# Logits of two router layers with their matrix as the weights on four column groups, and an earlier load of the memory matrix

## The chip, the cores and the metric

One NeuronCore of a Trainium2 chip runs the whole program. The metric is the time of one execution in microseconds on the device; lower is better. TensorE (PE in the rows, its weight loads PEld) multiplies, VectorE (DVE) and ScalarE (ACT) empty PSUM and do the element work, GpSimd (POOL) works on SBUF alone, and SyncE (SP) issues most DMAs.

## What is computed

An attention with a memory read, then two mixture-of-experts layers, each with one expert for a token. All is float32. There are 4 batches of 576 positions, 8 heads of width 64, so 2304 tokens of width 512, 8 experts with a hidden width of 1024.

```python
a = softmax(causal(q @ k.T / 8));  local = a @ v
q_p = where(q > 0, q, exp(q) - 1) + 1
mem = (q_p @ M_prev) / (q_p @ z_prev + 1e-6)
x = g * mem + (1 - g) * local            # g = sigmoid(beta), per head

def moe(x, l, w1, w2):                   # l: the logits of 8 experts
    e = argmax(l, axis=1); gate = softmax(l)[e]
    return gate * (relu(x @ w1[e]) @ w2[e])
# layer 1: l = (x/|x|) @ (emb/|emb|).T / tau;   layer 2: l = x @ w_gate
```

## The kernel before, in words

**Attention.** The work goes by 16 pairs of heads (4 batches times 4 pairs), each cut into 10 units. A loop over units writes out by hand what every engine does in each of them; tables of events (`ev_pe` for TensorE, `ev_ew` for the others) are filled ahead with functions under unit numbers, 10 units to a pair. Within a unit the elementwise events come before the scores, these before the TensorE events. Every engine runs its own instructions in the order written, so that a place in a table is a place in each queue. `load_mz` (line 76) puts the memory matrix and its normalizer into the tile `mz`: a GpSimd memset and four DMAs on SP. It stands under unit -4. `scale_v` (line 108) multiplies the first pair's values by 1 - g on GpSimd, under unit -7, and has to wait for their DMA and for the gate. `mscale` (line 174) then scales the first pair's block of `mz` on GpSimd, and `M` (line 181) is the matmul with it into `psm`.

**Logits of the first layer.** While a later pair is computed, the finished rows of a batch are transposed to `xT` (four blocks of 128 features, by 512 or 640 tokens). For batches 0 to 2 `lg_pe` (line 1054) forms their logits: for each tile of 128 tokens (4, 5 and 4 of them) four matmuls, one for each block of features, with the block of `xT` as the weights (128 by 128) and 8 columns of the scaled matrix `enT` streaming. They are put in two places, units 10 and 11 behind a batch's base. The last batch is done apart (`part_pe`, `last`) and is not touched.

**The experts.** A step is one tile of up to 128 rows of one expert. `step` (line 1342) writes it by hand: a first product into `ph0` and `ph1`, a ReLU, transposes (`hT`), a second product into `py` (24 matmuls). Operands are split in a high and a low float32r part (`hilo`: an ACT copy and a DVE subtraction), weights too (`splits`), whenever the next expert's weights come in. In a step of the first layer TensorE also routes the rows that the step before has put out: `yT_pe` (line 1269) transposes them into `pm0`, `yT_ev` copies them to `hs[0]` on ACT, `logits_pe` (line 1264) makes their logits of the second layer with four matmuls (again the rows as weights, 8 columns of `wgT` streaming), and `route2` turns these into an expert and a gate on DVE. Between the layers `chain1` (line 1615) does the same for the last step, interleaved with the first step of the second layer by the numbers in `n1`.

## Time and profile before

| | us |
|---|---|
| median of 3 runs (lowest, highest) | 925.56 (925.24, 927.02) |
| profiled execution, its own time | 926.38 |
| its span, first to last instruction | 924.6 |
| TensorE busy in it | 894.5 (97%) |
| VectorE, ScalarE, GpSimd busy | 494.9, 482.3, 269.8 |

The profile follows one execution. A busy share is an average over the whole span, so stretches are read apart: the timeline gives the start and length of single instructions or of runs of equal ones, a view by stretches gives the busy time of every engine and the granted clock of TensorE (1.00 is 2.4 GHz, 0.50 is 1.2 GHz). A float32 matmul that is no transposition stands in the records as two weight loads and two matmuls.

### The profile page before, as it was taken

The numbers are of one execution on the slowest core, as the hardware profiler recorded it, in microseconds if no ns is written. First come the engines' busy times: TensorE is split into PE (matmuls) and PEld (weight loads), VectorE is DVE, ScalarE is ACT, GpSimd is POOL, SyncE is SP. The second block draws the span as 40 slices with busy tenths as digits, with TensorE's granted clock in tenths as the row PEclk, the third lists the DMA queues.
The fourth block names the chain that finished last, engine by engine and source line by source line (L and its number), as shares of the span: only waits on it lengthen the run. The fifth ranks groups of instructions, "written<-read, shape, count | busy, mean of one in ns | idle before, by whom it ended". The sixth has DMA issues, their size and how long they took to land. (4 is left out here: it accounts for less than half of the span.)

```text
span 924.6 us, 20884 instructions
## 1 busy us (share of the span) xinstructions
PE 894.5 (97%) x5351; PEld 713.9 (77%) x5351; DVE 494.9 (54%) x1563; ACT 482.3 (52%) x969; POOL 269.8 (29%) x370
## 2 busy tenths in 40 slices
PE   5999999999999999999999999998999999999996
PEld 2777777787777878887888888886868888888885
DVE  3565675556575685369635576543567314463430
ACT  3566666646755835467434463532266434564531
POOL 3364744526434102211222212121131212221221
PEclk9899999979999999999999999999999999999999
DMA  6311433413305245438523416111657514384111
GB/s 130 73 41 40 124 115 90 121 21 72 86 14 195 80 148 201 133 116 303 174 96 115 139 47 207 60 48 39 228 193 277 186 47 130 121 298 144 42 36 39
DMA packets 102437, 110.31 MB, mean 119 GB/s; under 512 B 69882, under 2 KB 69882, under 8 KB 102276
## 3 DMA queue, kind: packets, MB, share of 16 engines
q1 hardware_dynamic: 94244, 85.33, 30.3%
q0 software_dynamic: 8032, 23.22, 7.6%
q8 instruction: 54, 0.88, 0.4%
q14 instruction: 107, 0.88, 0.3%
HBM read 90.32 MB, written 19.25 MB: 119 GB/s over the span
## 5 line engine op out<-in xcount | busy, mean ns | idle before, releaser
L1226 PE MATMUL py<-Wh,b 128*128 (+1 forms) x688 | 243.3, 409 | 2.2 <-DVE b L1170 2.1
L1226 PE MATMUL ph<-Wh,b 128*128 (+1 forms) x672 | 230.6, 404 | 0.6 <-ACTq L1237 0.6
L920 DVE TENSOR_TENSOR Wl<-stg,Wh 128x1024 f32 (+1 forms) x120 | 145.3, 1224 | 87.1 <-ACT Wh L917 81.4
L1226 PEld LDWEIGHTS py<-Wh,b 128*128 128x128 f32 x688 | 129.5, 188 | 30.0 <-DVE b L1170 3.7
L1226 PEld LDWEIGHTS ph<-Wh,b 128*128 128x128 f32 x672 | 126.9, 189 | 29.7 <-ACTq L1237 1.0
L917 ACT ACTIVATE Wh<-stg 128x1024 f32 (+1 forms) x120 | 125.7, 1058 | 23.8 <-DVEq L1237 7.5
L1226 PE MATMUL py<-Wl,b 128*128 (+1 forms) x344 | 135.8, 395 | 0.0
L1226 PE MATMUL ph<-Wl,b 128*128 (+1 forms) x336 | 133.4, 397 | 1.2 <-DVEq L1237 1.2
L1170 DVE TENSOR_TENSOR b<-pt,b 128x512 fp32r<-128x512 f32 x86 | 59.4, 690 | 112.4 <-ACT b L1169 112.0
L287 ACT ACTIVATE att<-psat 128x512 f32<-128x512 f32 (+1 forms) x144 | 66.7, 463 | 88.5 <-PE psat L285 87.6
L308 PE MATMUL psav<-vb,att 128*128 128x128 f32 (+1 forms) x640 | 96.6, 282 | 0.9 <-ACT att L287 0.8
L308 PEld LDWEIGHTS psav<-vb,att 128*128 128x128 f32 x640 | 81.8, 192 | 12.4 <-issue 4.3
L1325 POOL DMA_INDIRECT out_dram<-ysb,xca x21 | 25.8, 1231 | 196.4 <-ACTq L1237 126.1
L1169 ACT ACTIVATE b<-pt 128x512 fp32r<-128x512 f32 x86 | 51.6, 600 | 53.8 <-PE pt L1330 41.3
L1226 PEld LDWEIGHTS ph<-Wl,b 128*128 128x128 f32 x336 | 63.7, 190 | 14.7 <-DVEq L1237 1.7
L1320 ACT ACTIVATE ysb<-py,xca 128x512 f32<-128x512 f32 x42 | 28.8, 687 | 88.1 <-PE py L1226 72.0
L1226 PEld LDWEIGHTS py<-Wl,b 128*128 128x128 f32 x344 | 65.0, 189 | 10.7
L233 DVE CUSTOM_DVE_ANT_0 a<-pss,wmask 128x128 f32<-128x128 f32 (+3 forms) x128 | 61.0, 485 | 21.4 <-PE pss L255 11.0
L268 ACT ACTIVATE a<-a,mx 128x128 f32<-128x128 f32 (+3 forms) x128 | 71.1, 556 | 0.4 <-DVE mx L233 0.3
L1135 POOL DMA_INDIRECT xg<-x_scratch,idx x48 | 55.2, 1150 | 39.2 <-POOL xca L1314 11.1
L1436 POOL DMA_DIRECT2D x_scratch<-xcb x21 | 11.9, 564 | 170.2 <-DVEq L1237 63.5
L285 PE MATMUL psat<-ident,a 128*128 128x128 f32 x320 | 58.1, 280 | 0.2
(370 smaller groups left out, 1309.1 us busy)
## 6 DMA issues: line engine op xcount, KB each, us to landing
stg<-in_moe_w_dram SPq DMA_DIRECT2D x120, 512.0 KB, 4.7
x_scratch<-ysb POOLq DMA_DIRECT2D x22, 256.0 KB, 2.7
qkn<-in_q_dram SPq DMA_DIRECT2D x32, 128.0 KB, 2.8
qkn<-in_k_dram SPq DMA_DIRECT2D x32, 128.0 KB, 2.9
vb<-in_v_dram SPq DMA_DIRECT2D x32, 128.0 KB, 2.6
x_scratch<-xb SPq DMA_DIRECT2D x16, 256.0 KB, 4.2
x_scratch<-stg SPq DMA_DIRECT2D x11, 258.0 KB, 3.0
xg<-x_scratch,idx POOLq DMA_INDIRECT x48, 4.1
```

What stands on the lines that cost most here:

```text
L233: nc.vector.tensor_tensor_reduce(out=out, in0=ps, in1=mask, scale=1.0, scalar=bound, op0=ALU.add, op1=ALU.min, accum_out=m)
L268: nc.scalar.activation(out=a[:, 0:N], in_=a[:, 0:N], func=AF.Exp, scale=-1.0, bias=mx, accum_out=rs_t[pi][:, c, j:j + 1])
L285: nc.tensor.transpose(ps[:, 128 * i:128 * i + 128], x, ident)
L287: nc.scalar.activation(out=att[:, 0:N], in_=ps[:, 0:N], func=AF.Copy)
L308: nc.tensor.matmul(av_t[pi][:, c, j:], att[:, 128 * kb:128 * kb + 128], vn[:, kb, j:, 0:D], start=(kb == 0), stop=(kb == c))
L917: return nc.scalar.activation(out=chunk(Wh, c, wv), in_=stg[:, c].unsqueeze(1), func=AF.Copy).ins
L920: return nc.vector.tensor_tensor(out=chunk(Wl, c, wv), in0=stg[:, c].unsqueeze(1), in1=chunk(Wh, c, wv).bitcast(F32), op=ALU.subtract).ins
L1135: return nc.gpsimd.indirect_dma_start(out=rows_of(t), out_offset=None, in_=rows, in_offset=bass.IndirectOffsetOnAxis(ap=idx[:, L, t:t + 1] ...
L1169: nc.scalar.activation(out=hi, in_=ps, func=AF.Copy)
L1170: nc.vector.tensor_tensor(out=lo, in0=ps, in1=hi.bitcast(F32), op=ALU.subtract)
L1226: mm = nc.tensor.matmul(ps, x[:, col:col + P], W, start=(first and q_ == qs[0]), stop=(last and q_ == qs[-1]))
L1320: nc.scalar.activation(out=ysb, in_=py, func=AF.Copy, scale=xc[:, 0:1])
```

## The change

Three things change. The tile `sel` (128 by 8) is new: a matrix of zeros with ones at rows 40 kk + e of column e, made once by five small GpSimd instructions in `setup_gates`.

First, both logits are made in two stages. The matrix, all four blocks of features by 8 experts (32 columns), is now the weights, and the rows stream: block kk of the rows (512 columns in the attention, 128 in a step) goes into the 32 PSUM partitions from 32 kk on. The 128 partitions so hold four times four parts, of which sel picks the four that belong, after they have been copied back to SBUF (ACT in the attention, over block 0 of `xT`; DVE in a step, over the first 128 columns of the transposed rows). A second matmul with that as weights and `sel` streaming adds them up. The fifth tile of batch 1 keeps the old way.

Second, in a step the transposes of the rows and their copy move ahead of the second half of the first product. Third, `load_mz` goes from unit -4 to unit -8.

```diff
-    ev_ew.setdefault(-4, []).append(load_mz)
+    ev_ew.setdefault(-8, []).append(load_mz)
...
+            nc.gpsimd.memset(sel, 0.0)
+            for kk in range(KD):
+                nc.gpsimd.affine_select(out=sel, in_=sel, pattern=[[-1, E]], compare_op=ALU.not_equal, fill=1.0, base=-(KD + 1) * E * kk, channel_multiplier=1)
...
-                sp = 2
-                for i in range(sp):
-                    pe(base + d - sp + i, lambda b=b, i=i, n=r.n: self.lg_pe(b, slot("pslg") if i == 0 else self.ps["lg"], tiles=range(i, n, sp)))
+                pe(base + d - 4, lambda b=b: self.parts_pe(b, slot("pslp")))
+                ew(base + d - 3, lambda b=b: self.parts_ev(b))
+                pe(base + d - 1, lambda b=b: self.sum_pe(b, slot("pslg")))
...
+        def parts_pe(self, b, ps):
+            self.ps["lp"] = ps
+            g = KD * E
+            for n in range(KD):
+                nc.tensor.matmul(ps[g * n:g * n + g], enT.rearrange("p k e -> p (k e)"), self.xT[b][:, n, 0:512], start=True, stop=True)
+        def parts_ev(self, b):
+            cp(1, self.xT[b][:, 0, 0:512], self.ps["lp"])
+        def sum_pe(self, b, ps):
+            self.ps["lg"] = ps
+            for i in range(4):
+                nc.tensor.matmul(ps[:, E * i:E * i + E], self.xT[b][:, 0, P * i:P * i + P], sel, start=True, stop=True)
+            if self.cols(b)[1] == 5:
+                self.lg_pe(b, ps, tiles=(4,))
...
+    def parts_pe(yT):
+        for kk in range(KD):
+            nc.tensor.matmul(pm0[KD * E * kk:KD * E * kk + KD * E, 0:P], wgT.rearrange("p k e -> p (k e)"), yT[:, P * kk:P * kk + P], start=True, stop=True)
+    def parts_ev(yT):
+        nc.vector.tensor_copy(yT[:, 0:P], pm0[:, 0:P])
     def logits_pe(yT):
-        for kk in range(KD):
-            nc.tensor.matmul(pm1[:, 0:E], yT[:, P * kk:P * kk + P], wgT[:, kk], start=(kk == 0), stop=(kk == KD - 1))
+        nc.tensor.matmul(pm1[:, 0:E], yT[:, 0:P], sel, start=True, stop=True)
...
         hT(0, b)
+        if rt2:
+            yT_pe()
+            yT_ev(b.hs[0])
...
-            next_rows(t + 1)
+            xT_pe(rows_of(t + 1))
         if rt2:
-            yT_pe()
-            yT_ev(b.hs[0])
+            parts_pe(b.hs[0])
+            parts_ev(b.hs[0])
+        if more:
+            hilo(psx, b.x)
+        if rt2:
             route2_iov()
...
         yield
+        parts_pe(b.hs[1])
+        parts_ev(b.hs[1])
+        yield
         logits_pe(b.hs[1])
...
-    C, n1 = chain1(), (1, 1, 1, 5, 1, 0, 2, 0, 4, 6, 0)
+    C, n1 = chain1(), (1, 1, 1, 6, 1, 0, 2, 0, 4, 6, 0)
```

Line numbers in the lists of the changed kernel are its own. First the SP queue from the first pair's values on (`vb`: values, `qkn`: queries and keys), before:

```order
L105 DMA vb_141<-in_v_dram 128x4x64 x2
L106 DMA vb_141<-in_v_dram 64x2x64
L105 DMA vb_142<-in_v_dram 128x4x64 x2
L106 DMA vb_142<-in_v_dram 64x2x64
L96 DMA qkn<-in_q_dram 128x4x64 x2
L96 DMA qkn<-in_k_dram 128x4x64 x2
L98 DMA qkn<-in_q_dram 64x2x64
L98 DMA qkn<-in_k_dram 64x2x64
L84 DMA mz<-in_M_prev_dram 64x16x64
L85 DMA mz<-in_z_prev_dram 64x16x1
L84 DMA mz<-in_M_prev_dram 64x16x64
L85 DMA mz<-in_z_prev_dram 64x16x1
```

The same stretch of the SP queue now:

```order
L105 DMA vb_142<-in_v_dram 128x4x64 x2
L106 DMA vb_142<-in_v_dram 64x2x64
L84 DMA mz<-in_M_prev_dram 64x16x64
L85 DMA mz<-in_z_prev_dram 64x16x1
L84 DMA mz<-in_M_prev_dram 64x16x64
L85 DMA mz<-in_z_prev_dram 64x16x1
L105 DMA vb_143<-in_v_dram 128x4x64 x2
L106 DMA vb_143<-in_v_dram 64x2x64
L96 DMA qkn<-in_q_dram 128x4x64 x2
L96 DMA qkn<-in_k_dram 128x4x64 x2
L98 DMA qkn<-in_q_dram 64x2x64
L98 DMA qkn<-in_k_dram 64x2x64
```

The four loads of `mz` pass the nine issues for pairs 1 and 2; on GpSimd their memset passes the first pair's `scale_v` likewise. Next TensorE in the attention, where batch 0 has its logits (`pst`, `pstr`: transposes of queries and keys, `psat`: of the weights of attention, `psm`: memory, `pss`: scores), before:

```order
L285 MATMUL psat<-ident,al_146 128x128 x4
L255 MATMUL pss<-kT,qT 128x512 x2
L136 MATMUL pst<-ident,qkn 128x128 x4
L1060 MATMUL pslg<-enT,xT 128x8 x8
L285 MATMUL psat<-ident,a 128x128
L285 MATMUL psat<-ident,al_146 128x128
L185 MATMUL psm<-mz,ph 128x130 x3
L1060 MATMUL pslg<-enT,xT 128x8 x8
L285 MATMUL psat<-ident,a 128x128
```

And now, from two units further ahead:

```order
L1074 MATMUL pslp<-xT,enT 32x512 x4
L308 MATMUL psav<-vb_144,att 128x128 x2
L185 MATMUL psm<-mz,ph 128x130
L185 MATMUL psm<-mz,ph 64x130
L308 MATMUL psav<-vb_144,att 128x64 x2
L285 MATMUL psat<-ident,al_147 128x128 x4
L255 MATMUL pss<-kT,qT 128x512 x2
L136 MATMUL pst<-ident,qkn 128x128 x4
L285 MATMUL psat<-ident,a 128x128
L285 MATMUL psat<-ident,al_147 128x128
L185 MATMUL psm<-mz,ph 128x130 x3
L1083 MATMUL pslg<-sel,xT 128x8 x4
```

Sixteen matmuls with 8 columns have become four with 512 columns onto 32 partitions each, right behind the transposes of `pstr`, and four with 8 columns. Last TensorE in a step of the first layer (`psx`: the next rows' transposes, `pm`: the tiles `pm0` and `pm1`, `hs`: transposed rows), before:

```order
L1226 MATMUL ph_4146<-Wh_4137,b_4238 128x512
L1165 MATMUL psx<-ident,xg_4235 128x128 x4
L1271 MATMUL pm_4150<-ident,ysb 128x128 x4
L1226 MATMUL py<-Wh_4138,b_4239 128x512
L1226 MATMUL py<-Wl_4140,b_4239 128x512
L1226 MATMUL py<-Wh_4138,b_4240 128x512
L1330 MATMUL pt_4148<-ident,hs_4233 128x128 x4
L1226 MATMUL py<-Wh_4138,b_4239 128x512
L1226 MATMUL py<-Wl_4140,b_4239 128x512
L1226 MATMUL py<-Wh_4138,b_4240 128x512
L1267 MATMUL pm_4145<-wgT,hs_4232 128x8 x4
L1226 MATMUL py<-Wh_4138,b_4239 128x512
```

And now:

```order
L1250 MATMUL ph_4142<-Wh_4133,b_4234 128x512
L1189 MATMUL psx<-ident,xg_4231 128x128 x4
L1292 MATMUL pm_4146<-hs_4228,wgT 32x128 x4
L1250 MATMUL py<-Wh_4134,b_4235 128x512
L1250 MATMUL py<-Wl_4136,b_4235 128x512
L1250 MATMUL py<-Wh_4134,b_4236 128x512
L1362 MATMUL pt_4144<-ident,hs_4229 128x128 x4
L1250 MATMUL py<-Wh_4134,b_4235 128x512
L1250 MATMUL py<-Wl_4136,b_4235 128x512
L1250 MATMUL py<-Wh_4134,b_4236 128x512
L1299 MATMUL pm_4141<-sel,hs_4228 128x8
L1250 MATMUL py<-Wh_4134,b_4235 128x512
```

The place of the rows' transposes (L1271) is taken by the four matmuls with 32 output partitions; the transposes themselves now stand six matmuls earlier, behind the first `hT`. At the old place of the logits one matmul is left of four.

## Rows read from the trace of the kernel before

**Rows 1.** The page, part 1: busy time of the engines, share of the span, instructions.
```profile
PE 894.5 (97%) x5351; PEld 713.9 (77%) x5351; DVE 494.9 (54%) x1563; ACT 482.3 (52%) x969; POOL 269.8 (29%) x370
```

**Rows 2.** Timeline of the start: us from the start, length, engine, line, operation, count [idle before, releaser].
```profile
14.71 1.82 POOL L78 MEMSET mz<- 128x2080 f32 x1
22.97 0.40 POOL L177 TENSOR_TENSOR mz<-mz,gt 128x128 f32<-128x128 f32 x1 [6.43 <-DMA mz<-in_M_prev_dram]
...
10.29 1.15 SPq L105 DMA_DIRECT2D vb<-in_v_dram  x2
...
18.76 1.06 SPq L85 DMA_DIRECT2D mz<-in_z_prev_dram  x1
...
18.80 0.38 PE L285 MATMUL psat<-ident,al 128*128 128x128 f32 x1
23.42 1.43 PE L185 MATMUL psm<-mz,ph 128*128 128x130 f32 x4 [4.24 <-POOL mz L177]
```

**Rows 3.** Stretches: us, busy (count) of PE, PEld, DVE, ACT, POOL, granted clock, DMA, GB/s.
```profile
22.43:29.25 6.82, 5.83 (x30) 3.84 (x30) 2.79 (x11) 0.98 (x3) 2.53 (x3) 0.50 0.62 131
114.59:118.00 3.41, 3.41 (x22) 2.32 (x22) 2.25 (x8) 1.10 (x4) 1.78 (x3) 0.50 0.00 0
186.27:196.51 10.24, 10.24 (x55) 8.82 (x54) 4.29 (x19) 2.91 (x9) 3.86 (x5) 0.50 0.03 6
```

**Rows 4.** Timeline of TensorE at the logits of attention's batches 0, 1 and 2.
```profile
109.95 1.92 PE L1060 MATMUL pslg<-enT,xT 128*128 128x8 f32 x16
...
119.78 0.49 PE L255 MATMUL pss<-kT,qT 64*128 64x256 f32 x2
...
183.11 2.74 PE L1060 MATMUL pslg<-enT,xT 128*128 128x8 f32 x24
...
196.95 0.70 PE L255 MATMUL pss<-kT,qT 64*128 64x256 f32 x4
...
259.25 1.92 PE L1060 MATMUL pslg<-enT,xT 128*128 128x8 f32 x16
...
267.57 0.70 PE L255 MATMUL pss<-kT,qT 64*128 64x256 f32 x4
```

**Rows 5.** Timeline of TensorE in one step, and all matmuls of L1267 (minimum, median, maximum ns).
```profile
396.06 0.40 PE L1226 MATMUL py<-Wh,b 128*128 x1
396.29 0.95 PE L1267 MATMUL pm<-wgT,hs 128*128 128x8 f32 x8
397.10 0.48 PE L1226 MATMUL py<-Wh,b 128*128 x1
397.42 0.39 PE L1226 MATMUL py<-Wl,b 128*128 x1
...
L1267 PE MATMUL pm<-wgT,hs x176: 170/256/256, 339.4 to 638.5; 128*128 128x8 f32 x176
```

**Rows 6.** Timeline of TensorE where scores of two heads run; 64*128: rows by columns used.
```profile
160.64 0.27 PE L285 MATMUL psat<-ident,a 128*128 128x128 f32 x1
...
160.84 0.49 PE L255 MATMUL pss<-kT,qT 64*128 64x128 f32 x4
161.16 0.22 PE L152 MATMUL pstr<-ident,qkn 64*128 64x64 f32 x1
...
156.66 0.46 PE L244 MATMUL pss<-kT,qT 64*64 64x288 f32 x2
...
156.96 0.41 PE L244 MATMUL pss<-kT,qT 64*64 64x288 f32 x2
157.30 0.33 PE L1039 MATMUL psxt<-ident,xb 128*128 128x128 f32 x1
```

**Rows 7.** All copies of the transposed rows on ScalarE (minimum, median, maximum ns).
```profile
L1274 ACT ACTIVATE hs<-pm x22: 598/604/607, 337.8 to 636.4; 128x512 f32<-128x512 f32 x22
```

**Rows 8.** Timeline between the layers: the first hT's low part, the ranks.
```profile
641.39 0.69 DVE L1170 TENSOR_TENSOR b<-pt,b 128x512 fp32r<-128x512 f32 x1 [1.55 <-ACT b L1169]
...
641.96 0.18 PE L1303 MATMUL pm<-oh,tri 128*128 128x8 bf16 x1
```

More of the change, by code (lines that the diff above doesn't have):

```diff
@@ L525, in tile_kernel @@
     wgT = cst.tile([P, KD, E], F32, name="wgT")
+    sel = cst.tile([P, E], F32, name="sel")
     rtau = cst.tile([P, 1], F32, name="rtau")
```

## The prediction

> **What bounds the kernel now.** I read the page's busy times first, then TensorE's idle times by releaser, then the granted clock by stretches, then the timeline around each edit. TensorE is busy 894.5 of 924.6 us [rows 1]. So an edit is worth what it takes off TensorE's queue, unless it falls into one of the few idle times, and work moved to the other engines, each busy half the time, is free as long as nobody waits for it. The largest idle time is at the start: 4.24 us before the first matmul with `mz`, released by the scaling of `mz` on GpSimd [rows 2]. Right behind it the clock is low: 0.50 of 2.4 GHz from 22.43 to 29.25 [rows 3]. Two more low stretches lie right behind the logits of batches 0 and 1: 3.41 us and 10.24 us [rows 3]. Behind those of batch 2, the same code, it stays high.
>
> **The earlier load of `mz`.** The scaling at 22.97 waited for a DMA, of which the last was issued at 18.76 [rows 2]: 4.2 us from issue to use. These issues stood behind nine others for pairs 1 and 2 that begin at 10.29, and behind the memset, which ran at 14.71 to 16.53 because it came after the first pair's scaling of values. Now the memset comes first; GpSimd has nothing else then and the values land later anyway, so it costs nothing there. The four issues begin near 10.3 and end near 13.5 (the sequence took 3.3 us with its gaps: 16.5 to 19.8). With 4.2 us to use, `mz` is scaled at some 17, and TensorE wants it at 19.2. The stall of 4.24 us goes, with 2 us to spare. What is late next: loads of pairs 1 and 2 come 3.3 us later, but pair 1's values are first used some 10 us behind this point, pair 2's queries later still. Bounds: 3.0 gained if the small packets of `mz` and the other loads delay each other by 3 us more, 4.24 if not. I take 4.2.
>
> The clock adds to it. TensorE stood still for most of 19.2 to 23.4, and the low stretch followed. Without the stall it has work throughout. In 22.43 to 29.25 it was busy for 5.83 us at half speed [rows 3]; at full speed that is 2.9 less. DVE and ACT then have to keep up with twice the pace directly, so I take 2.0, bounds 0 and 2.9. Sum of this edit: -6.2.
>
> **What one logits matmul costs now.** In a step two matmuls of the second product start at 396.06 and 396.29, 0.23 apart; with eight records of the logits behind, the next two start at 397.10 and 397.42 [rows 5]. 397.42 - 396.06 less two intervals of 0.23 is 0.90 us: 0.112 for each record. Eight columns don't take that long; the load of 128 weight columns does. In the attention sixteen records from 109.95 on take the same per record [rows 4].
>
> **What streaming costs.** No row shows column groups side by side; the nearest are the scores, where two heads use different halves of the array [rows 6]. Four records of 128 columns from 160.84 to 161.16 take 0.32; two of 288 take 0.30 (156.66 to 156.96), and the second of each two starts within 0.01 of the first: two lengths ("x2, 0.46") that one record alone would have. Solving both: 0.11 us for 128 streamed columns, 0.43 for 512, 0.10 for a load of 128 weight columns, 0.05 for 64, and so some 0.03 for 32. Also: between a transposition (0.11 itself) and the first of these pass 0.20, and 0.34 from the last pair of 288 (0.25 itself) to the next transposition: 0.09 for each change of the array's form.
>
> **A step.** Two records stay for the last matmul, 0.22; saved 0.67. The four new matmuls, if the groups run side by side in two rounds: 0.09 + 0.03 + 2 x 0.11 + 0.02 of stagger + 0.09, and the next weights' load in the open, 0.11: 0.56. Net -0.11, and 176 records are 22 such places [rows 5], 21 of them in steps: -2.3. If groups run one after another it is eight rounds for two, +0.66, net +0.55.
>
> DVE's copy of 128 columns is below ACT's 0.60 for 512 [rows 7]; between it and its reader stand six matmuls and four transposes of TensorE, 6 x 0.23 + 0.4 = 1.8 us, so it is hidden. The moved transposes cost TensorE the same. Their ACT copy now stands between the high part of the first `hT` and the ReLU of `ph1`: both copies are 0.60 each, some 1.6 with the hand-overs, while TensorE has the four transposes, six matmuls and the next rows' transposes, 2.3. Hidden with 0.7 to spare, less in steps where ACT also copies weights; there I allow 0 to 0.5 each. Queued behind that copy is only the ReLU, which has to wait for `ph1` anyway.
>
> **Between the layers.** Here the logits come half a product later than before. Ranks start at 641.96, and DVE spends 641.39 to 642.08 on the low part of the first `hT` [rows 8]; the second half of the expert's choice now falls behind that. TensorE would wait until about 642.5. With 0.34 more for the matmuls less what is saved: +0.5 in place of -0.1, bounds 0 and 1.
>
> **The attention.** Batch 0 had 32 records, 3.58. Now `pslp` stands behind `pstr`, which already has its own form, so that one change of form is new: 0.09 + 0.03 + 2 x 0.43 + 0.02 = 1.00; then eight records, 0.90. Saved 1.68, the same for batch 1 (its fifth tile stays) and 2: -5.0. Side by side or not decides here too: eight rounds for two are +2.6 a batch. ACT's new copy, 0.60 [rows 7], comes three times beside other work; the added PSUM buffer is freed by it two units before its next user. The five small GpSimd instructions stand on no path.
>
> From the first logits to the same score matmul pass 8.32 us in batch 2, 9.83 in batch 0 and 13.84 in batch 1 [rows 4]; batch 1 has eight records more, 0.90. So the low clock costs 1.5 and 4.6 us. What TensorE did before each fall was long series of 8-column matmuls. In their place come 0.9 us of streaming and half or less of these; batch 2 had as much and kept its clock. I take -5.0 of the 6.1, bounds 0 and 6.1.
>
> The Trainium skill speaks of such groups twice, and the sum above uses neither. TensorEngine Tiling (Array Packing), Key Properties, says that tiles work independently, weight loads too; TensorE: Matmul & The Clock Gate, Measured speedup vs the span model, has 2.38 times for three column tiles. As an estimate from that page, four groups would take 2.5 rounds, not 2: 910 in place of 908. No row here can show it.
>
> **Sum.** -6.2 - 5.0 - 5.0 - 2.3 + 0.5 = -18.0. The profiled execution took 926.4, so 908.4; it is 0.8 over the median of the runs, so 907.6 to 908 for a median.
>
> **Rivals.**
>
> Groups in order of the program. Each float32 matmul is two records. If a group may start only when the group before has begun its second record, four matmuls take five rounds, not two: +0.33 in 22 places is 7.3, +1.3 in three is 3.9: 919. Against it: with two heads the second one's first record starts within 0.01 of the first one's [rows 6]; but these use other rows of the array, not the same rows and other columns. The page TensorE: Matmul & The Clock Gate of the Trainium skill says in The mechanism that matmuls start and end strictly in order; the trace disagrees for the two heads if their records were queued matmul by matmul, and says nothing of columns.
>
> Slower: the groups don't overlap at all, since all four use every row of the array. Then each of the eight records streams its columns alone. +0.66 in 22 places is 14.5, +2.6 three times is 7.7: 930. A round more costs 22 x 0.11 + 3 x 0.43 = 3.7 in all, so a step alone gains only up to three rounds, and the whole change is slower from 2 + 18.0 / 3.7 = 6.9 rounds on. For it: no row shows such an overlap. Against it: two heads with 64 by 64 blocks do overlap.
>
> Less from the clock and the start: falls come elsewhere, or DVE and ACT can't keep up behind the start. Taking 1 of the 7 us of clock: 914.
>
> The moved copy is late: 10 steps with weights coming in at 0.5 each: 913.
>
> **Chances.** Forecast 0.50 (alone 903 to 912), less clock 0.20, late copy 0.05, program order 0.13, no overlap 0.12. Low end: full clock gains (1.1 and 0.9 more), full overlap and one of the other low stretches gone: 904, with the runs' scatter 903. High end takes in the program order: 920. This leaves out the 930 and little else. A measurement of this kernel tells about 0.2% from no change, 923.7 to 927.4; faster 0.86, same 0.02, slower 0.12.
>
> **What would show it.** Right: the wait for `mz` gone from TensorE's list and 1.00 in 22 to 29; four records of L1292 starting within some 0.03 of each other, then four more 0.1 later; the stretch of batch 1 near 7 us and at 1.00. Wrong: L1292 or L1074 in starts 0.1 or 0.4 apart (program order: five, no overlap: eight); a wait of L1292 for the ACT copy; waits for pair 1's or 2's loads in place of that for `mz`.

## The result, and the profile after

The changed kernel takes **905.28 us** (904.48 to 906.16), the kernel before 925.86 (925.24 to 927.02): a ratio of 0.9775, 95% interval 0.9759 to 0.9790. Forecast were 908, with 903 to 920. The profiled execution spans 903.2 us, 21.3 less than 924.6. The total is near the forecast by luck, since its errors cancel: in the runs with these parts alone (below) both kinds of logits brought 4.6 us where the sum had 11.8, the earlier load brought 9.4 where it had 6.2, and 7 us came from something that the prediction has no term for.

The page, part 1, beside [rows 1]: TensorE lost 24 us of busy time.

```profile
PE 870.2 (96%) x5347; PEld 686.9 (76%) x5347; DVE 502.1 (56%) x1585; ACT 483.8 (54%) x972; POOL 275.3 (30%) x375
```

Where the 21.3 us went, from the starts of the same matmuls in both traces (us; the small rest lies between the stretches named):

| stretch | before | after | gained | forecast |
|---|---|---|---|---|
| start to the first scores of pair 1 | 34.54 | 26.01 | 8.5 | 6.2 |
| pair with the logits of batch 0 | 22.04 | 20.15 | 1.9 | 2.9 |
| the same, batch 1 | 25.83 | 21.17 | 4.7 | 5.4 |
| the same, batch 2 | 20.51 | 21.14 | -0.6 | 1.7 |
| first layer, third step to the last | 286.44 | 283.65 | 2.8 | 2.3 |
| between the layers (one step) | 17.25 | 18.75 | -1.5 | -0.5 |
| second layer to the end | 275.89 | 270.66 | 5.2 | 0 |

(The forecast's 5.0 for the clock is shared over batches 0 and 1 as 1.5 to 4.6, which is how the prediction read the falls there.)

Three rows depend on what one execution did. At batch 2, one DVE instruction was held up for 1.0 us (below); in four other runs with the same attention code it was not, and the pair took 19.9, a gain of 0.6. The last two rows share a fall of the clock. In the kernel before, the clock is low for 3.41 us between the layers and for 3.41 more at 691.4, inside a step of the second layer that takes 15.65 there, and 14.1 in the runs below whose tiles lie alike and whose clock stays high there. The changed kernel has one low stretch of 6.83 between the layers instead. So some 1.5 of the 5.2 in the last row belongs with the -1.5 above it. Of the 14 traces of this document ten have the one long stretch and four the two short ones, with the old routing and with the new.

**The start**, beside [rows 2]. Timeline of the start in the changed kernel, GpSimd, SyncE's queue and TensorE:

```profile
6.05 1.82 POOL L78 MEMSET mz<- 128x2080 f32 x1
...
16.92 0.40 POOL L177 TENSOR_TENSOR mz<-mz,gt 128x128 f32<-128x128 f32 x1 [2.11 <-DMA mz<-in_M_prev_dram]
...
10.36 0.60 SPq L84 DMA_DIRECT2D mz<-in_M_prev_dram  x1
...
17.48 0.82 PE L185 MATMUL psm<-mz,ph 128*128 128x130 f32 x4
```

The memset stands at 6, the issues run from 10.36, the scaling comes at 16.92, and the first matmul with `mz` has no wait ahead of it. No load of pair 1 or 2 is waited for in its place. Of the 8.5 us, 1.7 are earned ahead of all this, as the same four transpositions show, in the changed kernel (first) and in the kernel before.

```profile
16.77 0.65 PE L136 MATMUL pst<-ident,qkn 128*128 128x128 f32 x4
```

```profile
17.68 1.12 PE L136 MATMUL pst<-ident,qkn 128*128 128x128 f32 x4
```

The trace's first record of full speed is at 13.9 here, and in the trace before at 19.0, just ahead of the stall. The 14 traces have it between 13.3 and 22.1 with the early load and between 14.1 and 29.9 with the late one, so these runs don't tie it to the change. It also used up the 2 us to spare of the forecast: the scaling ended at 17.32, and TensorE came for it at 17.48.

**The clock**, beside [rows 3]. Stretches of the changed kernel (busy time and count of PE, PEld, DVE, ACT, POOL, granted clock, DMA share, GB/s): the start, the pairs of batches 0 and 1, and one of the low ones that are left.

```profile
22.43:29.25 6.82, 6.82 (x55) 5.11 (x53) 4.13 (x18) 4.58 (x14) 1.11 (x3) 1.00 0.59 132
97.30:113.00 15.70, 14.67 (x121) 10.66 (x120) 12.29 (x53) 9.33 (x28) 9.66 (x15) 1.00 0.26 58
164.20:185.30 21.10, 19.89 (x164) 14.80 (x163) 15.04 (x60) 11.65 (x34) 8.22 (x9) 1.00 0.21 47
...
614.60:621.40 6.80, 6.03 (x15) 4.18 (x15) 0.23 (x1) 0.60 (x1) 1.03 (x2) 0.50 0.14 45
```

In 22.43 to 29.25 TensorE now does 55 matmuls at 1.00 where it did 30 at 0.50. Behind the logits of these batches the clock no longer falls.

**Four column groups**, in one step, beside [rows 5]. Four windows end later and later at the same place, so that the records of L1292 can be told apart: they hold one, four, five and all eight of them.

```profile
380.37 0.27 PE L1189 MATMUL psx<-ident,xg 128*128 128x128 f32 x1
380.57 0.30 PE L1292 MATMUL pm<-hs,wgT 128*32 128x128 f32 x1
...
380.57 0.32 PE L1292 MATMUL pm<-hs,wgT 128*32 128x128 f32 x4
...
380.57 0.41 PE L1292 MATMUL pm<-hs,wgT 128*32 128x128 f32 x5
...
380.57 0.43 PE L1292 MATMUL pm<-hs,wgT 128*32 128x128 f32 x8
380.93 0.50 PE L1250 MATMUL py<-Wh,b 128*128 x1
```

Four records together last 0.02 longer than one alone, the fifth begins some 0.13 behind the first, and eight last 0.02 longer than five. So all four groups run side by side, in two rounds. From the last transposition to the next product pass 0.56 us, as forecast.

**The new waits in the attention**, beside [rows 4]. TensorE's timeline at batch 0 (first three rows, `pslp` and its end), then its waits at batches 0, 1 and 2:

```profile
97.14 0.28 PE L152 MATMUL pstr<-ident,qkn 64*128 64x64 f32 x2
97.35 1.06 PE L1074 MATMUL pslp<-xT,enT 128*32 128x512 f32 x8
98.34 0.49 PE L308 MATMUL psav<-vb,att 128*128 128x128 f32 x2
...
105.88 0.30 PE L305 MATMUL pslo<-vb,att 128*64 128x65 f32 x2 [0.76 <-DVE m L627]
...
180.60 0.43 PE L308 MATMUL psav<-vb,att 128*128 128x64 f32 x2 [0.94 <-ACT att L287]
...
248.59 1.35 PE L305 MATMUL pslo<-vb,att 128*64 128x65 f32 x20 [0.70 <-DVE m L627]
...
251.84 0.44 PE L308 MATMUL psav<-vb,att 128*128 128x64 f32 x2 [1.04 <-ACT att L287]
```

From `pslp`'s first record to the next matmul pass 0.99 us, as forecast (1.00). But TensorE now stands still behind the logits: 0.76 at batch 0, 0.94 at batch 1, 0.70 and 1.04 at batch 2. DVE at batch 2, in the kernel before and now, shows what the removed matmuls had covered:

```profile
262.58 0.56 DVE L204 TENSOR_TENSOR memx<-psm,rn 128x384 f32<-128x384 f32 x1
263.85 0.19 DVE L622 TENSOR_REDUCE m<-pslg 128x4 f32<-128x32 f32 x1 [0.70 <-PE pslg L1060]
```

```profile
247.89 0.56 DVE L204 TENSOR_TENSOR memx<-psm,rn 128x384 f32<-128x384 f32 x1
248.36 0.18 DVE L627 TENSOR_REDUCE m<-pslg 128x4 f32<-128x32 f32 x1
```

Before, DVE read `psm` while the second series of 8-column matmuls ran, and then waited 0.70 us for the logits. Now the logits are there from 246.87 on, but DVE has no pause, is still reading `psm` at 247.89 and takes up the logits at 248.36. What stands behind the wait of 1.04, on DVE, GpSimd and ACT:

```profile
248.80 1.22 DVE L631 SCALAR_TENSOR_TENSOR t<-d,ioer 128x32 f32<-128x32 f32 x1
...
250.28 0.97 DVE L635 TENSOR_TENSOR oh<-t,km 128x32 bf16<-128x32 f32 x1
251.18 0.18 DVE L649 TENSOR_TENSOR d<-d,sc 128x32 f32<-128x32 f32 x1
...
248.82 2.38 POOL L168 TENSOR_TENSOR ph<-ph 128x576 f32<-128x576 f32 x2
...
251.39 0.23 ACT L650 ACTIVATE d<-d 128x32 f32<-128x32 f32 x1 [3.94 <-DVE d L649]
251.53 0.26 ACT L287 ACTIVATE att<-psat 128x128 f32<-128x128 f32 x1
```

It reads upwards: TensorE's `psav` waits for ACT's copy `att`; that stands in ACT's queue behind the tanh of the gates (L650); the tanh waits for DVE's choice of the expert (L627 to L649); and of that choice the instruction L631, 32 columns wide, takes 1.22 us, beside two GpSimd instructions of 2.38 together. In the trace before the same instruction takes 0.19 to 0.20 all four times. Of the eight traces with the new logits, three have it at 1.22 at batch 2 and five at 0.19; at batch 1 it takes 1.20 to 1.21 in seven of them. The run with the steps of before shows the place again (below).

### The profile page after: what moved, and what is told of

It reads as the page before. It is cut to its first block, busy times and chain, and to the rows that moved or that the text cites. A ratio compares the mean times of both kernels' runs of the same rounds, so it can differ in the third digit from the quotient of the medians.

```text
span 903.2 us, 20913 instructions
## 1 busy us (share of the span) xinstructions
PE 870.2 (96%) x5347; PEld 686.9 (76%) x5347; DVE 502.1 (56%) x1585; ACT 483.8 (54%) x972; POOL 275.3 (30%) x375
## 5 line engine op out<-in xcount | busy, mean ns | idle before, releaser
L1250 PE MATMUL py<-Wh,b 128*128 (+1 forms) x688 | 240.8, 406 | 2.6 <-DVE b L1194 2.4
L1250 PE MATMUL ph<-Wh,b 128*128 (+1 forms) x672 | 226.7, 398 | 0.5 <-ACTq L1261 0.5
L1250 PE MATMUL ph<-Wl,b 128*128 (+1 forms) x336 | 131.1, 390 | 2.7 <-DVEq L1261 2.7
L1474 POOL DMA_DIRECT2D x_scratch<-xcb x21 | 11.9, 566 | 162.1 <-DVE xcb L1332 59.4
```

The lines of the kernel that those rows point to most:

```text
L1250: mm = nc.tensor.matmul(ps, x[:, col:col + P], W, start=(first and q_ == qs[0]), stop=(last and q_ == qs[-1]))
```

## The experiments

The first three runs ask what the places of tiles in SBUF have to do with the result, the next three what each part is worth alone. Behind the result of each stand its lowest and highest time and the ratio to the kernel before on the same chip.

**An unused tile of 32 bytes**, put into the kernel before where `sel` lies in the changed one, so that the tiles allocated behind it on the same side of SBUF lie 32 bytes further.

```diff
+    pad = cst.tile([P, 8], F32, name="pad")
+    nc.gpsimd.memset(pad, 0.0)
     rtau = cst.tile([P, 1], F32, name="rtau")
```

> The kernel before, plus an unused tile of 8 floats (one memset on GpSimd) where the changed kernel has sel, so that every SBUF tile allocated behind it, the weights of the experts among them, lies 32 bytes higher, as in the changed kernel. Theory of addresses: the steps of the second layer, in which the change alters no instruction and which went from 12.50 to 12.29 us, became faster by where the weights lie. Then they take 12.29 here too, the steps of the first layer 13.74, and the whole some 917 (925.9 less 41 steps of 0.21). Rival: the shorter steps come from the changed instructions or from that one execution: 12.50 and 926.

Measured: 919.52 (918.81 to 920.94), 0.9924 [0.9905, 0.9943]. A step of the second layer falls from 12.50 to 12.28, a plain step of the first (the length that most of them have) from 13.95 to 13.78. Not one instruction of them has changed. What has moved are the large matrices `Wh` and `Wl`, which stream through TensorE: they lie at 0 modulo 64 bytes in the kernel before, and at 32 here and in the changed kernel. The operands that TensorE loads as weights (`x0`, `b0` to `b5`) are allocated from the other end and lie at 32 in all three.

**The same with 64 bytes** (16 floats).

> The same with 16 floats: 64 bytes. Theory of addresses with a period of 64 bytes: as the kernel before, steps of 12.50 and 926. With a longer period, or if any shift helps: 12.29 and 917. Rival without addresses: 926.

Measured: 926.65 (925.32 to 930.97), 1.0011 [0.9996, 1.0025]; steps 12.50 and 13.95 as before, and the large matrices at 0 again. So it is the place, not the tile. Of the first 18 starts in one second-layer step, these are the first and the last, in the kernel before, in the changed one and in a later run (below):

```profile
779.36 0.40 PE L1226 MATMUL ph<-Wh,b 128*128 x1
...
783.33 0.39 PE L1226 MATMUL ph<-Wh,b 128*128 x1
```

```profile
772.35 0.39 PE L1250 MATMUL ph<-Wh,b 128*128 x1
...
776.20 0.40 PE L1250 MATMUL ph<-Wh,b 128*128 x1
```

```profile
774.59 0.39 PE L1226 MATMUL ph<-Wh,b 128*128 x1
...
778.45 0.40 PE L1226 MATMUL ph<-Wh,b 128*128 x1
```

The 17 intervals take 3.97, 3.85 and 3.86 us: 0.2335 each in the kernel before, 0.2265 and 0.227 in the other two.

**The changed kernel at the old places** (a further 32 bytes, so that the large tiles lie as before modulo 64).

```diff
     sel = cst.tile([P, E], F32, name="sel")
+    pad = cst.tile([P, 8], F32, name="pad")
+    nc.gpsimd.memset(pad, 0.0)
```

> The changed kernel plus an unused tile of 8 floats, so that with sel everything lies 64 bytes higher than in the kernel before. Theory of addresses with a period of 64 bytes: the second layer's steps back at 12.50, the first layer's at 13.85, in all 905.3 + 8.6 = 914. Rival: 12.29 and 905.

Measured: 912.99 (912.70 to 913.33), 0.9850 [0.9833, 0.9866]. Second-layer steps are back at 12.50; a plain first-layer step takes 13.83. So all that the diff speaks of is worth 13.9 us by the ratio (12.4 to 15.5) of the 20.8, and the place the other 7. The run also isolates the routing: 13.95 to 13.83 is -0.12 for a plain step, forecast -0.11.

**The earlier load alone.**

```diff
-    ev_ew.setdefault(-4, []).append(load_mz)
+    ev_ew.setdefault(-8, []).append(load_mz)
```

> The kernel before with load_mz at unit -8, nothing else. Theory: the stall of 4.2 us and the low clock behind it go, pair 1's first scores come 8.5 us earlier as in the changed kernel, in all 917.4. Rival of a smaller share: in the changed kernel's execution the clock had risen earlier, at 13.9 and not 19.0, for a reason of that execution; then 6.2 and 919.7. Rival that the rest of the attention gives it back: 925.

Measured: 916.53 (915.54 to 920.28), 0.9899 [0.9871, 0.9928]. Pair 1 begins 8.1 us earlier, and it is kept to the end.

**The attention's logits alone**, at the old places: the changed kernel with `load_mz` and the steps' routing as before, and the 32 bytes.

```diff
-    ev_ew.setdefault(-8, []).append(load_mz)
+    ev_ew.setdefault(-4, []).append(load_mz)
...
-        nc.tensor.matmul(pm1[:, 0:E], yT[:, 0:P], sel, start=True, stop=True)
+        for kk in range(KD):
+            nc.tensor.matmul(pm1[:, 0:E], yT[:, P * kk:P * kk + P], wgT[:, kk], start=(kk == 0), stop=(kk == KD - 1))
```

> Only the logits of the attention are changed (with a tile of 8 floats beside sel, so that all lies 64 bytes higher, which was shown to cost nothing); load_mz and the steps are as before. Theory of the cover: TensorE saves 1.68 us at each of three batches, and loses it again within the next units in waits for VectorE (the choice of the expert) and ScalarE (its tanh, behind which the copies of the attention's weights stand); what stays is the clock, which no longer falls behind the logits: 3 to 6 us, 920.5 to 923.5, and between the first scores of the pair before batch 2's logits and of the pair behind, the time is 20.5 to 21.2 as before or longer. The forecast's sum: 5.0 more, 915.5 to 918.5, and 18.8 for that stretch.

Measured: 921.10 (918.95 to 925.04), 0.9947 [0.9929, 0.9965]. The three pairs gain 1.9, 4.6 and 0.6, with waits for DVE's m of 0.77 and 0.69 and one for `att` of 0.94. Three traces with the old logits have no fall of the clock at batch 0, and the pair takes 20.52 in them, for 20.15 here: of the 1.68 that leave TensorE's queue, 0.37 leave the span. The clock behind the logits is shown by this run and the one before it. Attention from batch 0's logits on, old logits (earlier load alone), then new:

```profile
95.00:282.00 187.00, 184.89 (x1473) 142.27 (x1471) 116.96 (x487) 115.26 (x326) 89.11 (x91) 0.97 0.33 93
```

```profile
95.00:282.00 187.00, 181.75 (x1471) 135.80 (x1472) 120.53 (x502) 122.80 (x347) 96.15 (x106) 1.00 0.35 98
```

In all six kernels with the old logits this stretch has a clock of 0.95 to 0.97, with the falls now behind one batch, now behind another; in the eight with the new ones it is 1.00 seven times and 0.99 once. Behind the last batch, whose 8-column matmuls stay, the clock falls in 13 of the 14 traces.

**The steps' routing alone**, at the old places (the changed kernel with the attention's logits and `load_mz` as before, and the 32 bytes).

> Only the routing in the steps is changed (at addresses 64 bytes higher); load_mz and the attention's logits are as before. Forecast: 22 times 0.11 less, 0.6 more between the layers: 924.6. Theory after the traces: the plain steps gain 0.12 each, but steps with weights coming in lose 0.4 to 1.6, so that nothing is left: 926.5, give or take 1.

Measured: 927.15 (924.01 to 929.48), 1.0003 [0.9987, 1.0020]. The plain steps take 13.82 to 13.84, so the routing does save. Of the steps with weights coming in, some grow (14.74 where 13.97 was, 14.39 where 14.01 was, 15.51 where 15.36 was) and one shrinks (14.81 where 15.20 was). From the third step to the second step of the second layer only 0.6 of 303.7 us is gained. As a whole the part makes no difference that can be told from noise.

**The tanh of the gates one unit later**, in the changed kernel.

```diff
-                ew(base + d, lambda g=g: next(g))
+                ew(base + d + 1, lambda g=g: next(g))
```

> The changed kernel with the first piece of the gates (a multiplication on VectorE and the tanh on ScalarE) one unit later. Theory of the cover: the waits of the value matmuls for ScalarE's copies, 0.9 and 1.0 at two batches, and of the next transposes, 0.27 each, came from the tanh that waits for VectorE in front of them; they go: 1.5 to 3 less than 905.3. Rival: VectorE itself is what is late, and the next wait takes their place: 905.3.

Measured: 905.41 (903.38 to 906.93), 0.9769 [0.9741, 0.9796], no other than the changed kernel. In its trace the three pairs together are 2.3 us shorter than in the changed kernel's (waits for `att` of 0.37, 0.74 and 0.22 in place of 0.94 and 1.04), but the clock fell once in a step, which took 17.54. Of the 2.3, some 1.2 can't be put down to the edit: L631 took 0.19 at batch 2 here, as it did in four runs without it. The waits of 0.77 and 0.70 for DVE's m stay: they have another cause.

**All four products of a step onto the same column group.** Everything else stays; four copies of 32 partitions take the place of DVE's one.

```diff
-            nc.tensor.matmul(pm0[KD * E * kk:KD * E * kk + KD * E, 0:P], wgT.rearrange("p k e -> p (k e)"), yT[:, P * kk:P * kk + P], start=True, stop=True)
+            nc.tensor.matmul(pm0[0:KD * E, P * kk:P * kk + P], wgT.rearrange("p k e -> p (k e)"), yT[:, P * kk:P * kk + P], start=True, stop=True)
...
-        nc.vector.tensor_copy(yT[:, 0:P], pm0[:, 0:P])
+        for kk in range(KD):
+            nc.vector.tensor_copy(yT[KD * E * kk:KD * E * kk + KD * E, 0:P], pm0[0:KD * E, P * kk:P * kk + P])
```

> The changed kernel, but in the steps the four matmuls write to the same 32 partitions, side by side in columns, so that they use one column group; four copies on VectorE bring them to their places. Theory of the forecast: the groups overlap, one group alone takes eight rounds of 0.11 instead of two: 0.66 more in each step, 14.30 in place of 13.64, 919.8 in all. Rival: the four overlap in one group too, or the rounds don't set the time: 905.3, or 1 more for the copies.

Measured: 918.66 (917.50 to 920.52), 0.9910 [0.9886, 0.9935]: a plain step takes 14.28 for 13.64, +0.64, where eight rounds for two were priced at +0.66. Its timeline, in windows that hold one, two and all eight records of L1292:

```profile
370.39 0.30 PE L1292 MATMUL pm<-hs,wgT 128*32 128x128 f32 x1
...
370.39 0.41 PE L1292 MATMUL pm<-hs,wgT 128*32 128x128 f32 x2
...
370.39 1.06 PE L1292 MATMUL pm<-hs,wgT 128*32 128x128 f32 x8
```

Here each record adds 0.11; on four groups the second to the fourth added 0.02 in all. With one group a plain step takes 0.50 more than with the old logits at the same places (13.78), with four it takes 0.14 less, so it is the groups that make streaming the rows pay there.

**`iov` later in the step.** One small DVE instruction moves behind the second `hT`, right ahead of the choice. The trace of the changed kernel had suggested it, at the step that grew most (15.36 where 13.97 was): TensorE's wait, and the chain before it on GpSimd and DVE.

```profile
362.06 0.50 PE L1250 MATMUL ph<-Wl,b 128*128 x1 [1.43 <-DVEq L1261]
...
354.43 0.18 POOL L1354 COPY xcb<-xca 128x4 f32<-128x4 f32 x1 [4.87 <-DMA x_scratch<-xcb]
...
354.65 0.23 DVE L1312 TENSOR_SCALAR iov<-ioer,xcb 128x8 f32<-128x8 f32 x1 [1.61 <-POOL xcb L1354]
...
357.59 3.50 DVE L925 TENSOR_TENSOR Wl<-stg,Wh 128x1024 fp32r<-128x1024 f32 x3 [2.03 <-ACT Wh L922]
```

```diff
-        if rt2:
-            route2_iov()
         s.gemm(1, py, lh, 0, 0, 3)
...
+            route2_iov()
             gen = route2(t - 1)
```

> The changed kernel, but in a step the small DVE instruction iov (expert numbers times the valid mark of the rows before) stands right ahead of the choice of the expert, and no longer ahead of the second product. Theory: the steps in which weights come in are long (15.4 at 358, 14.8 at 401, 15.4 at 416) because iov waits on DVE for GpSimd's copy of xcb, which waits for the store of the old xcb; since all in DVE's queue is in order, the low part of the second hT, the split of the weights and so the next step's first matmuls are late. Then iov no longer holds anything, these waits of TensorE (1.43, 0.90, 1.46) lose at least 1 us each in two of them, and the whole is 2 to 3 us shorter than the changed kernel: 902.3 to 903.3. Rival: the weights' own transfers or splits set these steps' lengths; then the waits stay and the time is 905.3.

Measured: 903.20 (901.87 to 909.90), 0.9742 [0.9721, 0.9763]. The number is in the theory's range, the reason isn't its own: of the three waits the first fell from 1.43 to 0.65, the others are 1.00 and 1.61 for 0.90 and 1.46, and the first layer's steps take 284.1 in its trace for 283.7. Two of three fall to the rival, and even the first isn't shown to hang on `iov` alone: in the run with the steps' routing alone, `iov` stands where it was, and this wait is 0.63. The trace is of the longest of its executions (909.90), so where the 2 us of the median come from can't be read in it. What the middle one waits for (this run, DVE and TensorE):

```profile
409.87 3.68 DVE L925 TENSOR_TENSOR Wl<-stg,Wh 128x1024 f32 x3
413.46 0.68 DVE L1194 TENSOR_TENSOR b<-pt,b 128x512 fp32r<-128x512 f32 x1
...
414.20 0.50 PE L1250 MATMUL py<-Wh,b 128*128 x1 [1.00 <-DVE b L1194]
```

DVE subtracts three blocks of weights without a pause, and only then the low part that the product needs. The kernel before waits at this place as well:

```profile
423.98 0.50 PE L1226 MATMUL py<-Wh,b 128*128 x1 [0.99 <-DVE b L1170]
```

So the wait at this place is not the change's, and it has not grown: with the routing of before in the changed kernel (the last run below) it is 1.14 and the step takes 15.20, in the changed kernel 0.90 and 14.81, here 1.00 and 14.93.

**Two places moved.** As the run before, and the sum for batches 0 and 1, with all behind it, two units later; the tanh one unit later.

```diff
-                d = 12 if last else 12
+                d = 12 if last else 14
-                pe(base + d - 4, lambda b=b: self.parts_pe(b, slot("pslp")))
-                ew(base + d - 3, lambda b=b: self.parts_ev(b))
+                pe(base + 8, lambda b=b: self.parts_pe(b, slot("pslp")))
+                ew(base + 9, lambda b=b: self.parts_ev(b))
...
-                ew(base + d, lambda g=g: next(g))
+                ew(base + d + 1, lambda g=g: next(g))
```

> As the run before, and in the attention the sum over the four parts for batches 0 and 1, with all that follows it, two units later (the four matmuls on column groups stay where they are), and for every batch the tanh of the gates one unit later. Theory: the logits' saving was lost because the PSUM buffer of pslo is that of the second psm, whose reader on DVE is late, and because ACT's tanh waits for DVE's choice and holds the copies that TensorE needs. With the sum behind pslo, pslo takes a buffer that was emptied long before. Then the waits of 0.76 and 0.70 for DVE's m go, and those of 0.94 and 1.04 for the att copy shrink as in the kernel with the tanh later: 2 to 4 us off the run before, 899 to 901. Rival: the waits only move on, to whatever DVE and ACT do later: as the run before, 902 to 903.

Measured: **901.08** (899.71 to 902.29), 0.9720 [0.9702, 0.9738], below the changed kernel's interval. At batch 0 (TensorE, DVE):

```profile
104.34 1.38 PE L305 MATMUL pslo<-vb,att 128*64 128x65 f32 x20
...
106.42 0.96 PE L1083 MATMUL pslg<-sel,xT 128*128 128x8 f32 x8
...
104.08 0.56 DVE L204 TENSOR_TENSOR memx<-psm,rn 128x384 f32<-128x384 f32 x1
```

`pslo` now starts right behind the scores, while DVE is still reading `psm` (to 104.64). Its buffer is another, so the first wait was the rotation of the pool's two buffers. From pair 1's first scores to the end of the three pairs the gain on the kernel before is 8.6 for the changed kernel's 5.9, with L631 held up at batch 2 in both. At batch 1 it now meets no GpSimd instruction and takes 0.20 for 1.21. Batch 2, whose place was left, still waits 0.69 and 0.99.

**The weight operands moved by 32 bytes instead**, in the kernel before: `x0`, `b0` to `b5` lie at 0 modulo 64, and the streamed matrices stay at 0.

```diff
     bufs = Bufs(lambda i: fp.tile([P, 512], F32R, name=f"b{i}") if i < 6 else hs_[i - 6])
+    pad = fp.tile([P, 8], F32, name="pad")
+    nc.gpsimd.memset(pad, 0.0)
```

> The kernel before with an unused tile of 32 bytes behind the operands that are loaded as weights in the products: their places move from 32 to 0 modulo 64 bytes, and the streamed large matrices stay at 0. If the interval of the products depends on whether both lie alike modulo 64, it now is as in the run with the first pad no longer: both alike is then the slow case only if alike means slow; before had 0 and 32 (12.50 for a second-layer step), the changed kernel 32 and 32 (12.28). Theory (both alike is fast): 12.28 here, 919. Rival (only the streamed matrices' own place counts, 32 is fast): 12.50, 926.

Measured, in one execution: 919.65, second-layer steps 12.28, the third fence of the product's starts above. So it isn't the matrices' own place: both operands at 0, or both at 32, are fast, and the streamed one at 0 with the loaded one at 32 is slow. The other mixed case was not run.

**The steps of before in the changed kernel.**

> The changed kernel with the routing in the steps and between the layers as before (four matmuls of 8 columns, transposes behind the first product), so that the attention's logits, the earlier load and the new places in SBUF are left. The forecast's sum has -2.3 + 0.5 for what is undone: 907.1. Theory from the run with the steps' part alone: it is worth nothing as a whole, since what it saves in plain steps is lost in those with weights and between the layers: 905.3 within 1.

Measured: 903.85 (903.03 to 904.97), 0.9752 [0.9733, 0.9770]: not slower than the changed kernel (0.9775), so the steps' new routing earns nothing as a whole, as the theory had it and the forecast did not. In the traces the routing gains 1.0 in the first layer's steps (283.7 for 284.7) and takes 18.75 for 17.88 between the layers; the latter varies, though, with the low clock there (16.88 in the run with `iov` later, whose code there is the changed kernel's). The first layer's 1.0 is a sum of unlike steps: 17 of the 20 gain 3.0 together, and three lose 1.9 (1.50 in the step at 358, 0.24 and 0.20 in two later ones, with waits of 0.22 and 0.26 that are new). Elsewhere this run is better by chance: in its trace batch 2 gains 0.6 where the changed kernel loses 0.6, with the same instructions there. Its DVE, GpSimd and TensorE at that place:

```profile
248.74 0.19 DVE L631 SCALAR_TENSOR_TENSOR t<-d,ioer 128x32 f32<-128x32 f32 x1
...
249.19 0.80 DVE L635 TENSOR_TENSOR oh<-t,km 128x32 bf16<-128x32 f32 x1
...
248.77 2.40 POOL L168 TENSOR_TENSOR ph<-ph 128x576 f32<-128x576 f32 x2
...
250.58 0.43 PE L308 MATMUL psav<-vb,att 128*128 128x64 f32 x2
```

DVE's L631 was 0.03 us ahead of GpSimd and took 0.19; in the changed kernel, 0.02 ahead, it took 1.22, as long as one GpSimd instruction there. The choice ended 1.3 us sooner, and the wait of 1.04 is absent. The Trainium skill (SBUF — State Buffer, "SBUF: two separate sides") says that DVE and GpSimd share a pair of ports, as an exclusive lock that whichever starts first holds for a whole instruction, where a DVE instruction with two SBUF inputs meets a GpSimd instruction that reads SBUF. These two traces agree on the blocking: in the changed kernel L631 ends at 250.02, and the first of the two GpSimd instructions at 249.98; here L635 ends at 249.99 and the first one at 249.94. In the 14 traces this instruction took 0.94 or more eleven times, and each time it ended some 0.05 behind a GpSimd instruction. They don't show that the earlier start decides: DVE's record starts 0.02 ahead in the changed kernel, which was blocked, and also 0.02 ahead in the changed kernel at the old places, which was not.

## Why the prediction was right, and where it was not

**The earlier load: right in kind, too small.** 6.2 were forecast, 8.5 came in the trace, 9.4 (6.6 to 11.9) with this part alone. The stall went as worked out (scaling at 16.9 for "some 17"): 4.24. From that first matmul to pair 1 pass 8.53 us for 11.12: 2.6 for the clock, inside the bounds 0 to 2.9 and over the 2.0 taken, since DVE and ACT did keep up (55 matmuls in the stretch where 30 were). The 1.7 that is left is the earlier rise of the clock ahead of both, which no run ties to the change.

**The clock behind the logits: right.** "What TensorE did before each fall was long series of 8-column matmuls" is borne out by the fourteen traces: six with the series, which fall, against eight without.

**The attention's logits: the step that failed.** TensorE did save the 1.68 per batch: `pslp` and the change of form cost what was forecast. But the sum took what leaves TensorE's queue for what leaves the span. With the clock, 10.0 were forecast for the three pairs; 5.9 came in this trace and 7.1 in four others, where L631 was not held up at batch 2, and 4.9 us of the whole (3.2 to 6.6) for this part alone. Two sentences fell. "The added PSUM buffer is freed by it two units before its next user": two buffers instead of one turned the rotation, so that `pslo` takes `psm`'s and waits for its reader on DVE, 0.76 and 0.70; shown by the run with the sum behind `pslo`. And "an edit is worth what it takes off TensorE's queue, unless it falls into one of the few idle times" left out what the removed matmuls had covered. Under those 3.6 us DVE read `psm` and stood ready when the logits came; now it has no pause, so the choice of the expert comes late, ACT's tanh waits for it, and the copies of `att` stand behind the tanh (0.94 and 1.04). The choice also slid onto GpSimd's long instructions, and one of its own took 1.22 for 0.19. Moving the sum and the tanh brought 2.7 of the 4.1 back.

**The groups: right.** Two rounds, neither five (the rival in program order, 919) nor eight (no overlap, 930). The estimate of 2.5 rounds from the Trainium skill (TensorE: Matmul & The Clock Gate, Measured speedup vs the span model) is not borne out: the four streams of a round cost one, with 0.02 of stagger.

**The steps: right for one, wrong for the sum.** A plain step gained 0.12 for 0.11. But the 21 were multiplied as though all were plain. Most with weights coming in gained too; half of the gain was lost in one of them, where `iov` waited 1.61 in DVE's queue for `xcb` and its store, and TensorE 1.43 behind it, and a little more in two others. The rival "the moved copy is late" looked for the loss in such steps, with ACT as the cause; in the one it was DVE's queue. Between the layers the wait that was named is there, 0.41 for 0.5. Most of the rest of the 1.5 in the table is the low clock, 6.83 us at one go here and twice 3.41 in the kernel before, the second time in the second layer. What decides between the two isn't settled.

**What was in no term: 7 us from places in SBUF.** `sel` is 32 bytes wide in every partition. The measured parts add up: 9.4 for the load, 4.9 for the attention's logits, -0.3 for the steps, 7.0 (5.3 to 8.8) for the place make 21.0, the whole change 20.8; each part is uncertain by some 2, so that they meet this closely is partly luck. Without the place it would have been 913.0, next to the 914 of the rival "Less from the clock and the start", but for another reason.

Open is why the operands' places matter; the runs show only where they lie and what it costs. Open too is what decides between DVE and GpSimd when they start within some hundredths of a microsecond; that it is the lock was not tried with a kernel of its own, but read from the traces.

## What to carry to other kernels

Before work is taken off the bound engine, look up which other engine's work lies under it: the span gains only what is left when that work becomes the wait, and a buffer more in a small pool changes who waits for whom. A saving per step holds for steps like the one that was looked at: here one unlike step took back half of what the others gained. And when a new tile shifts what is allocated behind it, compare an instruction that has not changed in both traces, far from the edit, before the gain is put down to the edit. A stretch of one trace can also differ by chance: look at the same stretch in the other runs whose code there is the same.

## What the hardware showed that was not expected

- A product of a 128 by 128 operand as weights and 512 streamed columns starts every 0.2335 us when the weights lie at 32 and the streamed operand at 0 modulo 64 bytes in SBUF, and every 0.227 when both lie at 0 or both at 32. Over the whole kernel this is 7 us of 926.
- Four float32 matmuls on four column groups, queued one after another, run as four records that start within 0.02 us, then four more 0.13 behind.
- A DVE instruction of 32 columns takes 0.19 us alone and up to 1.22 beside a GpSimd instruction of 1.16, and where both start within 0.02 us it came out both ways.
- At the start TensorE works at half pace (1.12 us for four transpositions, 0.65 later) where the stretch's granted clock reads 1.00. The traces hold no record of the clock there, and a stretch without a record reads 1.00; the first record comes between 13.3 and 29.9 us in the 14 traces.
